# A hand-ordered program with a rewritten task order: 2736 tasks, the same work, another list

## The chip, the cores and the metric

The kernel runs on one core of one Trainium2 chip. The metric is the device time of one execution in microseconds (us), the median of the timed runs. A profile of one more execution shows every instruction on the engines: TensorE (PE for its matmuls, PEld for its weight loads), VectorE (DVE), ScalarE (ACT), GpSimd (POOL), and SyncE (SP), which issues nearly all DMAs.

## The reference

Two blocks in a row, in float32. The first is a recurrence over 768 steps for each of 4 x 8 heads with a 40 x 40 state; the second is a feed-forward layer on its output.

```
for t in range(768):
    y[t] = r[t] @ state
    Sa = state @ a[t]
    state = state * w[t] - outer(Sa, b[t]) + outer(v[t], k[t])
x = y as (3072, 320)
h = x @ w_in                       # 320 -> 2048
out = (h * sigmoid(1.702 * h)) @ w_out   # 2048 -> 320
```

## The kernel before

The sequence is cut into 12 chunks of 64 steps, and the batch into two pairs, which gives 24 units; unit i belongs to chunk i // 2. Within a unit the recurrence becomes matrix work. Cumulated decays come from matmuls (`ps_cum`, `ps_cumc`) or, from unit 4 on, from two scans on DVE (`sums`, L535). Score matrices follow (`ps_A`, `ps_RV`, `ps_N`), then the inverse of a triangular 64 x 64 matrix per head. It takes five `ps_level` steps in a row: a matmul, a copy W (L756), a subtraction E (L758), a 32 x 32 transpose ES (L707) and a spread EX (L716), which feeds the next level. Two corrections (`ps_Q`, `ps_T`), the right-hand sides `ps_B`, the solution `ps_X` and the output `ps_y` come next. `ps_zT` and `ps_rz` carry the state from unit i - 2. The outputs x of the two units of a chunk are written to DRAM (`part_with`, L964) and read back transposed (`get_back`, L970) as xT.

The feed-forward layer takes a chunk when its xT is there: 40 tasks `ps_up` (L1097), a GELU on ACT for each group of ten, and 16 tasks `ps_down` for most chunks. The last two chunks have a product with fewer multiplications (`ps_fast`, L997). The weights arrive as 64-bit words and are first turned into float32 on ACT, DVE and POOL (`weight`, L436): 8 pieces in four DMAs each. That is done during the first 95 us.

What sets the order of all this is a list written into the program. Each piece of work is a task, added by `plan.add` with the engines that it may run on. `ORDER` (L109 to L249) lists all 2736 tasks. An entry such as `113p1` says: task 113, on PE (p; a, d, g and s are ACT, DVE, POOL and SP), and, for a task that uses PSUM, bank pair 1 of four. `Plan.listed` (L89) walks through the list, and `rwkv7_gelu_quick` then emits the tasks one by one (L1169 to L1171). So the list sets four things: the order in which each engine takes its instructions, the engine of each task that may run on several (an EX spread may run on POOL, DVE or ACT), the order of the loads and stores on SP, and the bank pair of each PSUM tile. Each engine runs its own tasks in the list's order; between engines there are only the waits that the data and the buffers need. A load waits on SP until its buffer is free, and everything behind it on SP waits with it. A matmul into a bank pair waits until the last reader of the pair's tile before it is done.

The names that the steps below use: the loads `ak`, `b`, `rv`, `RV`, `time` of a unit (L500), `logw` and `wc` (L495); ahT and khT are the products L624 and L629 of ak with the decays, L626 is that of b, and kh and bh are L632; crossed copies Tc are L804. All matmuls have line L305, that of a helper.

Of the kernel before, what the change touches and what calls it, by code (L numbers as in the profile page):

```python
# [112 lines left out]
344s 92a 115d1 265p2 165d3 114a1 21d 273s 166p1 22d 35s 264p0 23g 116p3 167d1 43s 266a2 36s 118d3 28a 168d1 117d3 169p1 268g  # L113
63s 267a0 270s 119p2 91s 170a1 278g 277s 33s 120d2 287a 122d2 121a 279d 124a2 126p0 171d1 288p3 127a0 31d 172p1 479s 123a2 29d
289a3 51s 125a2 42s 30d 44s 128p2 173a1 45s 129d2 32g 174d1 134p0 175p1 135d0 275s 179a1 290d3 136p2 37a 280g 176d1 180d1 177d
181a1 186p0 291d 138a2 282g 276s 269s 137a2 178d1 146s 281g 187a0 38d 182p1 188p2 183a1 292p0 39d 139d 184p1 283p3 293a0 140s
185d1 284d3 189a2 343s 148a 285p2 315d 46a 190p3 286d2 335p1 141s 191d3 147s 347s 47d 334p2 192p3 61s 336a1 48d 294d0 194a3
348g 338d 337a2 195d 357a 295p2 351g 316p1 297d2 196s 318a1 349d 317a1 62s 296a2 319p1 193d3 358p0 40d 298p3 197s 360d0 41g
346s 361d 299a3 60s 54s 359d0 362p2 341a 300d3 385d 301p3 320a1 350g 364d2 323p1 303d3 355p0 363a2 352g 302a3 356d0 271a 386p3
324d1 365p2 388a3 321p0 64a 387d3 325d1 49d 304p3 322a0 478s 367d2 209p1 50g 309a3 53s 353p0 339s 307d3 210p1 211p1 354d0  # L120
308a3 212p1 366a2 310d3 213p1 305d3 470p0 214p1 272d 72s 368p3 340s 52s 198p2 69s 342d 369a3 215p1 71s 199p2 306a 200p2 370d3
216p1 471a 201p2 65d 202p2 389p3 66d 472a0 474s 217p1 476a 560s 390d3 371p0 67d 482s 218p1 70s 203p2 373d0 68g 219a1 204p2
205p2 477d 220p3 206p2 221p3 222p3 55a 311p1 223p3 80s 224p3 79s 312a1 225p3 372a0 207p2 56d 313p1 226p3 208a2 485d 374p0
314d1 227p3 58d 379a0 228p3 378a0 229p3 57d 326p2 230a3 375d0 59g 393p1 327d2 376a 391p3 394d1 231p2 392a3 558s 232p2 395d1
73a 233p2 81s 483d 381p3 475s 328p1 382a3 76d 380a0 473d 242p3 74d 377a0 481s 492a 78s 75d 243p3 480s 486d 77g 234p2 329d1
244p3 330d1 383p1 245p3 384d1 531d 82a 488p0 487g 235p2 489d0 236p2 237p2 331d 238p2 239p2 396p0 83d 332s 240p2 85d 562s 532p1
708s 241a2 246p3 397d0 559s 534a1 247p3 484d 533a1 84d 535p1 490p0 536a1 86g 398p2 491d0 706s 572a 550p1 253p0 399d2 551a 555s
400d2 561s 254p0 333s 401d 255p0 402s 552a1 564d 493p2 554s 556a 567g 570p1 494d2 705s 248p3 563d 566g 403s 249p3 495d2 498d
571d1 565g 256p0 250a3 496a2 251d3 696p1 497g 557d 539p2 252s 537p3 257p0 538a3 704s 540d2 553d 258p0 701s 611d 697a 499d
573p3 259p0 576a3 784s 574d3 260p0 700s 710d 787s 541d2 261a0 575d3 404p2 698a1 578d 405p2 577g 579d 568p3 711g 500p1 406p2  # L130
569d3 501a1 407p2 262d0 580p3 702a 502d1 408p2 263s 582d3 409p2 503d 410p2 583d 612p0 504a 411p2 584g 613d0 412p2 614d0 413p2
505p1 709d 414a2 426p0 427p0 506d1 428p0 507d1 429p0 699d 430p0 581d3 615p1 703d 431p0 616a1 785s 585p2 432p0 586a2 508d 433p0
434p0 509a 587d2 435p0 588d 448p3 589d 436a0 510p1 590p2 511a1 449p3 592d2 512d1 591a2 415p0 513d 416p0 593d 514a 417p0 594g
418p0 515p1 419p0 516a1 595p2 420p0 517d1 596a2 421p0 518d 422p0 597d2 519a 423p0 598d 424p0 599d 520p1 425a0 437p2 521d1
438p2 523d1 522g 439p2 524d1 440p2 525d1 441p2 442p2 526d1 527p0 718p1 528a0 443p2 719d1 929s 444p2 720d1 529p0 445p2 721d1
446p2 530d0 600p1 723d 447a2 542p0 722d 724g 603d1 604d1 619p2 543d0 605a1 450p3 620a2 606d1 544p0 621d2 601d1 602d 617p2 707s
546d0 451p3 618a2 783s 712d 547g 713d 607p1 725p2 608a1 452p3 609p1 453p3 548s 610d1 727d2 454p3 932s 726d2 622p1 728d 545d0
729a 775p2 455p3 623d1 780s 776a 549s 756d 730p0 624p1 456d3 457d3 731d0 458s 459p3 777a2 778g 732d0 786s 788g 781a 626d1 779s
460p3 625d1 627g 733d 795p2 835d 734a 461p3 735p0 791g 628s 462p3 796d2 736a0 792g 737d0 716p1 738d 463p3 782d 739g 1011s
920p2 757p0 925s 464p3 717d1 758a0 629s 790d 759a0 465p3 789d 740p1 466p3 741a1 921a 742d1 797p0 467d3 760p1 1008s 468d3 800a0  # L140
923d 652p3 761d1 469s 922a2 653p3 926a 798d0 714p2 930s 799d0 654p3 802d 924s 801g 655p3 934d 803a 656p3 836p1 657p3 715d2
658p3 659p3 837d1 762p0 838d1 927d 660p3 763a0 661p3 764p2 662a3 743d 630p1 744d 928s 631p1 765d2 632p1 766d2 804p0 633p1
805a0 634p1 635p1 806d0 745p3 807d 636p1 808a 748d3 637p1 933g 749d3 839p2 750d3 638p1 840a2 1009s 751d3 639p1 935g 809p0
746d3 640a1 641p2 810d0 642p2 793p3 747a 811d0 674p1 812d 794d3 813a 752p0 643p2 753a0 814p3 644p2 815a3 754p0 645p2 816d3
646p2 755d0 647p2 817d 767p3 818a 841p0 768d3 648p2 842a0 649p2 819p3 650p2 820a3 769p0 651a2 821d3 822d 823d 675p1 931s 771d0
824p3 770d0 772g 676p1 936d 827a3 828a3 942p2 829a3 677p1 1153s 830a3 945a2 937d 663p0 773s 825d3 664p0 1156s 943d2 665p0 826a
944d2 999p3 666p0 947d 946g 1000a 1004s 940p2 980d 667p0 948g 774s 668p0 941d2 669p0 670p0 831p2 671p0 1001a3 1002d 1003s
832d2 672p0 1005a 1013d 678p1 673a0 1006d 833p3 843p2 679p1 834d3 1007s 844d2 938p3 845d2 680p1 939d3 846p0 681p1 847d0 949p2
1012g 682d1 848p3 950a2 683d1 1014d 684s 685p0 849d3 1015g 1010s 850d3 1021p1 1016g 951d2 686p0 1024a1 1232s 851d 981p3 1235s
687p0 982a3 952d 852s 1022d1 983a3 953g 1144p2 1023d1 688p0 1026d 1145a 1149s 1025d 1027g 984p3 1059d 689p0 1154s 954p1 853s  # L150
985a3 1147g 690p0 1158d 1148s 955a1 986p3 1146a2 956d1 1150a 957d 691p0 958d 987a3 1151d 988p2 692p0 989a2 1152s 990d2 959p1
693a0 865p3 960a1 694d0 866p3 867p3 695s 961d1 868p3 962d 1028p2 963d 869p3 1029a2 870p3 1157g 871p3 1030d2 1060p0 1031d 872p3
1159d 1032a 873p3 1062d0 874p3 1033p1 1061a0 854p2 875a3 1035d1 855p2 1036d 856p2 1037d 1063p0 857p2 1064d0 858p2 1034a1 964p3
859p2 965a3 1038p0 860p2 966d3 1039a0 861p2 967d 1017p1 1040d0 968a 1041d 862p2 1018d1 863p2 1042g 969p3 864a2 876p0 970d3
# [1098 lines left out]
```

## Time and profile before

| what | value |
|---|---|
| timed runs | 673.79, 675.92, 680.55 us; median 675.92 |
| profiled execution | 673.46 us, of which the span from first to last instruction is 671.7 |
| first matmul, first `ps_up`, end of the last matmul | 3.7, 68.2, 667.8 us |
| granted TensorE clock, mean | 0.991 |
| PE, DVE, ACT, POOL busy | 644.0, 470.7, 318.4, 191.9 us |
| DMA | 69.78 MB, mean 104 GB/s |

The page gives busy time of each engine, and views of the trace cut it by stretches of time, list who waited for whom, and follow the chain of work that ended last. The time of a stretch matters more than the share of the whole: the first 72 us, in which weights load and the first four units have no feed-forward work beside them, differ from the rest.

### The profile page before, as it was taken

What the parts mean: (1) busy time and instruction counts of PE and PEld (TensorE: products, weight loads), DVE (VectorE), ACT (ScalarE), POOL (GpSimd) and SP (SyncE); (2) the same over time, 40 slices, a digit from 0 to 9 for tenths busy, and PEclk for the clock granted to TensorE, in tenths of its full rate; (3) what the DMA queues carried; (4) which work ended last, traced back from release to release, by engine and by line L of the source; (5) the groups of instructions that cost most, each with busy time, mean ns of one, the idle gap of its engine ahead of it and who ended that gap; (6) DMA issues with size and microseconds to landing.
All of it is one profiled execution on the core that took longest, in us unless ns stands there. A gap on an engine that the chain in (4) does not pass through costs nothing.

```text
span 671.7 us, 42976 instructions
## 1 busy us (share of the span) xinstructions
PE 644.0 (96%) x19872; PEld 566.4 (84%) x19872; DVE 470.7 (70%) x956; ACT 318.4 (47%) x658; POOL 191.9 (29%) x214
## 2 busy tenths in 40 slices
PE   5767999999999999999999999999999999999997
PEld 4656988999999898888888888789899787788997
DVE  5688986767867668757775886776757766676505
ACT  3566755534564664574455445454252344353020
POOL 4434344225123123123213620263322333003100
PEclk9699999999999999999999999999999999999999
DMA  7776836205314314432404413422322330210200
GB/s 234 248 239 193 254 125 199 78 14 156 109 45 139 114 43 121 126 112 70 128 14 127 137 48 103 123 67 72 114 86 69 95 90 15 81 44 11 67 21 22
DMA packets 35475, 69.78 MB, mean 104 GB/s; under 512 B 5472, under 2 KB 14816, under 8 KB 35296
## 3 DMA queue, kind: packets, MB, share of 16 engines
q1 hardware_dynamic: 35056, 66.87, 33.0%
q8 instruction: 156, 2.56, 1.5%
q10 hardware_dynamic: 240, 0.16, 0.1%
q14 instruction: 23, 0.19, 0.1%
HBM read 59.15 MB, written 7.86 MB: 100 GB/s over the span
## 4 chain that ended last, share of the span: by engine, by line
PE 93%; DMA 3%; DVE 2%; ACT 1%; issue 1%; SPq 0%; ACTq 0%; DVEq 0%
PE ps_up L305 31%; PE ps_down L305 26%; PE ps_level L305 9%; PE ps_y L305 5%; PE ps_fast L305 5%; PE ps_B L305 4%; PE ps_X L305 3%; PE ps_A L305 2%; PE ps_rz L305 2%; PE ps_N L305 2%; PE ps_RV L305 2%; PE ps_zT L305 1%; DMA time<-in_time 1%; DMA ak<-in_ak 1%; PE ps_cum L305 1%; PE ps_T L305 1%
## 5 line engine op out<-in xcount | busy, mean ns | idle before, releaser
L305 PE MATMUL ps_up<-xT_all,w_sb 64*64 64x256 f32 x3840 | 246.1, 377 | 0.2 <-PE ps_rz L305 0.2
L305 PE MATMUL ps_down<-w_sb,g 64*64 64x320 f32 x2560 | 201.3, 430 | 0.0
L305 PEld LDWEIGHTS ps_up<-xT_all,w_sb 64*64 64x64 f32 x3840 | 167.6, 133 | 17.7 <-DVE B L899 0.5
L305 PEld LDWEIGHTS ps_down<-w_sb,g 64*64 64x64 f32 x2560 | 114.0, 133 | 28.6 <-issue 0.3
L1107 ACT ACTIVATE g<-ps_up 128x1024 f32<-128x1024 f32 x48 | 49.1, 1026 | 62.2 <-PE ps_up L305 61.9
L756 ACT COPY W<-ps_level 128x512 f32<-128x512 f32 x56 | 32.7, 587 | 67.1 <-PE ps_level L305 53.0
L714 POOL TENSOR_TENSOR EX<-ES,quads 128x512 f32<-128x512 f32 x29 | 38.0, 1310 | 92.5 <-DVE ES L707 77.7
L305 PEld LDWEIGHTS ps_level<-W,EX 64*64 64x64 f32 x2560 | 56.8, 134 | 5.3 <-ACT EX L712 0.2
L758 DVE TENSOR_TENSOR E<-two,ps_level 128x256 f32<-128x256 f32 x80 | 33.3, 417 | 38.7 <-ACT W L756 22.6
L305 PE MATMUL ps_level<-W,EX 64*64 64x64 f32 (+1 forms) x2560 | 54.3, 217 | 0.0
L712 ACT ACTIVATE EX<-ES,quads 128x256 f32<-128x256 f32 x74 | 33.7, 503 | 35.8 <-DVE ES L707 31.1
L624 POOL TENSOR_TENSOR ak<-ak,FT 128x512 f32<-128x512 f32 x17 | 22.0, 1297 | 80.0 <-DMA ak<-in_ak 59.3
L305 PEld LDWEIGHTS ps_level<-PT,EX 64*64 64x64 f32 x1280 | 32.5, 144 | 9.1 <-issue 2.7
L305 PE MATMUL ps_level<-PT,EX 64*64 64x64 f32 (+2 forms) x1280 | 34.6, 242 | 5.5 <-DVE EX L728 2.0
L707 DVE STREAM_TRANSPOSE ES<-E 128x256 f32<-128x256 f32 x80 | 35.0, 441 | 4.1
L305 PE MATMUL ps_y<-M,bh 64*64 64x104 f32 (+1 forms) x768 | 35.2, 247 | 0.7 <-issue 0.4
L305 PE MATMUL ps_y<-RV,kh 64*64 64x104 f32 (+1 forms) x768 | 34.9, 247 | 0.2 <-issue 0.2
L912 DVE TENSOR_TENSOR M<-ps_X,later 128x832 f32<-128x832 f32 (+1 forms) x24 | 23.8, 991 | 12.1 <-PE ps_X L305 12.0
L896 ACT COPY B<-ps_B 128x416 f32<-128x416 f32 (+1 forms) x29 | 14.5, 498 | 37.1 <-PE ps_B L305 37.0
L305 PEld LDWEIGHTS ps_y<-RV,kh 64*64 64x64 f32 x768 | 28.5, 133 | 2.0 <-issue 0.4
L714 POOL TENSOR_TENSOR T<-ES,quads 128x512 f32<-128x512 f32 x9 | 11.5, 1277 | 64.6 <-DVE ES L707 64.6
L305 PEld LDWEIGHTS ps_B<-RV,A 64*64 64x64 f32 x768 | 24.7, 135 | 5.2 <-issue 1.2
(156 smaller groups left out, 1205.0 us busy)
## 6 DMA issues: line engine op xcount, KB each, us to landing
rv<-in_rv SPq DMA_DIRECT2D x48, 160.0 KB
ak<-in_ak SPq DMA_DIRECT2D x48, 160.0 KB
time<-in_time SPq DMA_DIRECT2D x24, 320.0 KB
xT_all<-x_dram SPq DMA_DIRECT2D x48, 160.0 KB
wc<-in_wc SPq DMA_DIRECT2D x20, 264.0 KB
logw<-in_w SPq DMA_DIRECT2D x24, 160.0 KB
RV<-in_v SPq DMA_DIRECT2D x24, 160.0 KB
b<-in_b SPq DMA_DIRECT2D x48, 80.0 KB
```

Source lines behind the costliest of these rows:

```text
L305: nc.tensor.matmul(o, lhsT, rhs, start=start, stop=True, skip_group_check=True)
L624: plan.add(R, {"DVE": 690.0, "POOL": 1270.0, "sbuf": True}, lambda t: of(t.engine).tensor_mul(ahT(), ahT(), FT_of(i)), reads=T("ak", "FT") ...
L707: plan.add(rank, dve(256), lambda t: nc.vector.transpose(ES(n), source(t)), writes=[key("ES", n, 6)], **reads)
L712: nc.scalar.activation(dst[:, :, h], ES(n), ACT.Copy, scale=quads[:, h, :1])
L714: of(t.engine).tensor_mul(dst, ES(n).unsqueeze(2).to_broadcast([128, 8, 2, 32]), quads.unsqueeze(1).to_broadcast([128, 8, 2, 32]))
L756: plan.add(rank, any2(512), lambda t: copy(t.engine)(tiles_of(W(n + 1)), blocks(psum(t, ""), 64)), writes=[key("W", n + 1, 5)], pair=pair)
L758: plan.add(rank, dve(256), lambda t: nc.vector.tensor_sub(tiles_of(E(n + 1)), every(two32, [128, 2, 4, 32]), blocks(psum(t, ""), 64)[:, :, ...
L896: plan.add(R, any2(4 * wide), lambda t: copy(t.engine)(dst(), some(psum(t, "")[:, :, :208])), writes=[("Bv", i)] if x and c > 0 else T("B" ...
L912: plan.add(R + 1, dve(8 * wide), lambda t: nc.vector.tensor_tensor(M_of(i)[:, :, :wide].rearrange("p (j b) n -> p b j n", b=2), some(psum( ...
L1107: plan.add(-45, {"ACT": 1030.0, "table": "gelu"}, lambda t: nc.scalar.activation(g_of(c * NQ + q).rearrange("p q b n -> p b q n"), psum(t, ...
```

## The change

Only the text of `ORDER` changes. It was searched for with the mean of six draws of late loads and scattered DMA packets as its target, and the words that came with it speak of units 4 to 22. The text differs from its first line to its last but a few entries. The first three lines of both:

```diff
-0s 7s 5s 8s 9s 6s 3a 88p3 16s 1s 87p1 100p2 89a3 12s 102a 95d 14s 90a1 93d 10s 101d2 98p3 97d 24s 94d 96d 103p1 11s 4a 99d3
-15s 132p0 105d1 17s 142p2 106d 143p3 133d0 13s 107p0 144a3 18s 2s 104a1 149g 109d0 130p1 34s 25s 108a0 26s 150d 158a 110p3
-145a2 131a1 152g 159p2 112d3 156p1 160a2 151g 111a3 161d2 162d 153d 19a 154p2 157d1 345s 163p3 155d2 27s 113p1 274s 164a3 20d
...
+0s 7s 5s 158a 8s 9s 6s 3a 87p3 1s 88p2 16s 89a2 10s 90a3 100p2 95d 102a 93d 12s 101d2 98p0 14s 97d 18s 94d 4a 99d0 103p2 11s
+96d 15s 132p0 105d2 142p1 17s 106d 104a2 143p2 133d0 24s 107p0 13s 144a2 2s 130p2 149g 109d0 34s 131a2 25s 108d0 145a1 151g
+26s 150d 110p0 153g 112d0 159p2 111a0 152g 156p1 160d2 19a 161d2 154p0 162d 345s 157d1 163p3 27s 274s 155d0 113p1 164a3 20d
...
```

Here 10 is the load of `ak` for unit 1, 12 and 14 its `rv` and `time`, 11 its `b`; 16, 15, 17 and 18 are the four DMAs of weight piece 0, and 24 is the first of piece 1; 149 and 151 are ahT and khT of unit 1, 150 is the product of its b, 152 and 153 are kh and bh; 108 and 111 are copies of unit 0's first levels, 159 is `ps_N` of unit 1 and 160 a copy of its result; 158 is the preset of unit 1 (L680).

Counted over the whole text: 303 tasks have another engine (DVE to ACT 99, ACT to DVE 86, DVE to POOL 50, POOL to DVE 39, ACT to POOL 18, POOL to ACT 11). 259 tasks have another bank pair. On PE 639 of 1076 tasks stand at another rank, on SP 204 of 269. DVE has 807 tasks in place of 831, POOL 165 in place of 147, ACT 419 in place of 413.

More of the change, by code (lines that the diff above doesn't have):

```diff
@@ L114 @@
[L114 to L130, printed above, removed]
@@ new lines @@
+1092p1 1198d2 1208p3 918d0 1093p1 1209a3 1378s 1196d2 1094p1 1095p1 1195a 1372s 1212p0 1200p2 1096p1 1213a0 1201d2 1210p3
+1214d0 1202p2 1097p1 1211a3 1376s 1203d2 1078p0 1229a 1373s 1098p1 919s 1215p2 1099a1 1241p3 1216d2 1079p0 1080p0 1242d3
+1081p0 1082p0 1217p1 1383d 1262p3 1219d1 1384g 1379s 1083p0 1084p0 1218d1 1385g 1111p2 1264d3 1112p2 1230d 1263a3 1085p0
+1086p0 1087p0 1220d 1388p3 1088a0 1113p2 1447p1 1283d 1114p2 1448a 1452s 1115p2 1389d3 1284p0 1265d 1116p2 1266d 1117p2 1122p3
+1285d0 1381d 1449a1 1451s 1118p2 1453a 1221s 1286d0 1119p2 1120p2 1287p0 1121a2 1123p3 1288d0 1267p0 1291p1 1222s 1269d0
@@ new lines @@
+1314p2 1413a1 1315p2 1308p0 1509a3 1414d1 1316p2 1415d 1317p2 1416d 1318p2 1486p1 1309p0 1488d1 1310p0 1489d 1487a1 1311p0
+1510d3 1490g 1319p2 1312a0 1417p1 1324p3 1422d1 1325p3 1418d1 1320p2 1423d1 1419g 1321p2 1322p2 1420a1 1326p3 1421d1 1323a2
+1491p0 1607g 1327p3 1492d0 1328p3 1329p3 1493d0 1424p1 1494d 1330p3 1425d1 1495g 1614p2 1331p3 1615d2 1825s 1332p3 1616d2
+1426p0 1333p3 1617a2 1427d0 1496p1 1334a3 1439p2 1500d1 1346p0 1497d1 1502d1 1498a 1440d2 1347p0 1619d 1441p2 1501d1 1499a1
+1503p1 1335p3 1442d2 1609g 1504a1 1336p3 1443d2 1337p3 1608g 1505p1 1511p2 1618g 1506d1 1348p0 1444d 1512a2 1681s 2425g 1349p0
@@ new lines @@
+1525s 1629d 1826s 1691p2 1613d1 1363p3 1692d2 1817a 1630d 1658p2 1660p1 1818a0 1830d 1820s 1364p3 1659a2 1824s 1661d1 1822a
+1537p0 1538p0 1365a3 1539p0 1366d3 1540p0 1662d1 1693p2 1631p3 1696a2 1904s 1541p0 1632a3 1694d2 1689p1 1907s 1695d2 1542p0
+1367s 1698d 1697g 1543p0 1690d1 1699a 1544p0 1545p0 1633d3 1546p0 1678d 1526p2 1547a0 1732p1 1700p3 1634d 1527p2 1635d 1528p2
+1529p2 1702d3 1530p2 1829d 1701a3 1531p2 1734a1 1819d 1532p2 1703d 1636p3 1733d1 1704g 1533p2 1638d3 1534p2 1639d 1637a3
+1535p2 1640d 1705p1 1536a2 1548p0 1707d1 1549p0 1708d 1735p3 1706a1 2422d 1709g 1550p0 1736a3 1551p0 1552p0 1641p1 1559p2
@@ new lines @@
+1856a0 1752p2 1753p2 1858d 1754p2 1589d3 1859a 1924p1 1590d3 1755p2 1955d 1591s 1860p0 1926d1 1761p3 1927d 1861a0 1756p2 1928g
+1757p2 1925a1 1862d0 1758p2 1863d 1759p2 2053g 1956p0 1760a2 1762p3 1958d0 1763p3 1764p3 1864g 1929p1 1765p3 1931d1 1766p3
+1932d 1865p2 1933d 1767p3 1870a2 1768p3 1930d1 1957a0 1769p3 1871d2 1934p1 1868d2 1770p3 1935a1 1794p0 1866d2 1771a3 1867g
+1936d1 1937d 1772p1 1869d2 1773p1 1938d 1959p2 1774p1 2054d 1960a2 2129s 1939p3 1775p1 1941d3 1776p1 1940d3 1872p2 1777p1
+1942d 2062p3 1873d2 1778p1 2055g 2427g 2426g 2064d3 1779p1 2063d3 1780p1 2065d3 1874p2 1781p1 1875d2 1783p3 1782a1 2047d
@@ new lines @@
+2183p2 1980p0 2184d2 2351s 2153p1 2279g 1981p0 2154a1 1986p3 1987p3 2155d1 1988p3 2156d 1989p3 2278d 2157a 1982p0 1983p0
+2079p1 1984a0 1990p3 2081d1 1991p3 2082d 1992p3 2080d1 2158p2 1993p3 2160d2 2083a 1996p1 2159d2 1997p1 1994p3 2267d 2161d
+2084p2 1995a3 1998p1 2086d2 1999p1 2162d 2000p1 2085a2 2001p1 2087d 2163p0 2088a 2018p2 2165d0 2166d 2089p3 2164d0 2002p1
+2093a3 2007p0 2008p0 2090d3 2003p1 2092d3 2091g 2004p1 2095d3 2005p1 2167d 2094a3 2019p2 2006a1 2277d 2009p0 2096p3 2010p0
+2097d3 2286p1 2098p3 2011p0 2289d1 2512s 2012p0 2099d3 1815s 2013p0 2287d1 2111p3 2288d1 2291d 2290g 2168p1 2014p0 2292g
@@ new lines @@
+2197s 2284p0 2295d2 2369g 2033p3 2285d0 2515s 2294a2 2028s 2296d 2330p0 2297g 2034p3 2331d0 2332p0 2367g 2402p2 2358g 2333d0
+2511s 2298p1 2404a2 2035p3 2403a2 2300d1 2513s 2301d 2036p3 2299d1 2302a 2334d0 2507p1 2303p2 2037d3 2508a 2198p0 2038d3
+2199p0 2305d2 2200p0 2306d 2509a1 2201p0 2307g 2304a2 2370p3 2202p0 2347a 2372d3 2203p0 2204p0 2371a3 2348d 2205p0 2206p0
+2405p3 2373d 2359p1 2406a3 2587s 2374d 2207p0 2209p2 2517d 2586s 2208a0 2210p2 2516d 2211p2 2039s 2212p2 2360d1 2375p3 2213p2
+2376d3 2214p2 2215p2 2377d3 2220p1 2378d 2221p1 2379d 2308p0 2216p2 2310d0 2380p3 2311d 2222p1 2382d3 2312a 2217p2 2309d0
@@ new lines @@
+2218p2 2223p1 2383d 2219a2 2313p0 2381d3 2384g 2224p1 2314d0 2225p1 2319a0 2226p1 2315g 2227p1 2317a0 2385p2 2318a0 2228p1
+2316a0 2387d2 2229p1 2388d 2386a2 2320p3 2525p0 2389g 2321a3 2242p2 2527d0 2230a1 2526d0 2231p3 2530d 2232p3 2528d0 2531g
+2233p3 2322p0 2234p3 2323d0 2390p1 2510g 2335p0 2394a1 2235p3 2393a1 2336d0 2236p3 2237p3 2238p3 2391d1 2337p0 2395d1 2392g
+2396a1 2239p3 2338d0 2519g 2514s 2240p3 2563d 2407p1 2241a3 2243p2 2339d0 2408a1 2520d 2340g 2409p3 2564p1 2410d3 2397p0
+2244p2 2398a0 2411d3 2566d1 2399p0 2529g 2245p2 2341s 2565a1 2400d0 2518g 2246p2 2523p3 2412p1 2342s 2247p2 2585s 2413d1
@@ new lines @@
+2610d 2542p1 2607a0 2641p3 2544d1 2433p2 2545d 2642a3 2434p2 2543d1 2435p2 2439p0 2546d 2611p1 2436p2 2613d1 2437p2 2614d
+2440p0 2438a2 2615d 2441p0 2442p0 2612d1 2443p0 2547p3 2616p1 2549d3 2444p0 2550d 2445p0 2618d1 2551a 2446p0 2548d3 2447p0
+2617a1 2448p0 2619d 2552p2 2620d 2449a0 2450p3 2553d2 2451p3 2557d2 2452p3 2554a 2594d 2621p1 2453p3 2558a2 2623d1 2559p0
+2555a2 2454p3 2624d 2556a2 2455p3 2560d0 2456p3 2625a 2622d1 2561p2 2457p3 2562d2 2626p1 2461p0 2630d1 2574p2 2629a1 2458p3
+2575d2 2459p3 2632a1 2462p0 2627d1 2460a3 2463p0 2631d1 2464p0 2645p2 2628a 2576p3 2646a2 2643p1 2647d2 2472d 2465p0 2644a1
```

209 lines of the change are left out of this document (93 added, 116 removed).

## The prediction

> **What bounds the kernel now.** I read the busy table first, then the stretches, then who waited for whom, then the chain that ended last.
>
> ```profile
> PE 644.0 (96%) x19872; PEld 566.4 (84%) x19872; DVE 470.7 (70%) x956; ACT 318.4 (47%) x658; POOL 191.9 (29%) x214
> PE 93%; DMA 3%; DVE 2%; ACT 1%; issue 1%; SPq 0%; ACTq 0%; DVEq 0%
> ```
>
> TensorE is busy 96% of the span, and 93% of the chain that ended last is TensorE. No other engine comes near. The stretches say where the other 4% lies:
>
> ```profile
> 0.00:25.00 25.00, 14.66 (x429) 13.17 (x433) 15.14 (x26) 10.28 (x29) 10.76 (x43) 0.93 0.80 253
> 25.00:45.00 20.00, 14.48 (x500) 13.00 (x492) 14.45 (x25) 12.36 (x32) 8.84 (x6) 0.83 0.76 233
> 45.00:72.00 27.00, 20.39 (x860) 18.42 (x861) 23.99 (x48) 17.92 (x40) 12.51 (x8) 1.00 0.61 186
> ...
> 300.00:350.00 50.00, 50.00 (x1565) 41.88 (x1561) 39.48 (x90) 24.21 (x47) 11.91 (x13) 1.00 0.27 81
> 350.00:400.00 50.00, 50.00 (x1504) 42.12 (x1500) 36.88 (x69) 24.09 (x43) 20.29 (x19) 1.00 0.37 103
> 400.00:450.00 50.00, 50.00 (x1590) 40.71 (x1584) 36.53 (x75) 26.67 (x60) 14.08 (x13) 1.00 0.31 88
> ```
>
> The columns are the stretch, its length, busy time of PE, PEld, DVE, ACT and POOL, the granted clock and the DMA share. TensorE idles 10.3, 5.5 and 6.6 us in the three stretches before 72 us. Ten stretches of 50 us from 100 to 600 us add up to 499 busy of 500. The waits of TensorE agree: the long ones (3.7, 3.0, 1.5 us) are all in the front.
>
> ```profile
> PE ps_cumc L305 <- POOL logw L372: 3.7, 1, 3.7
> PE ps_A L305 <- DVE ak L624: 3.0, 1, 3.0
> PE ps_level L305 <- DVE EX L728: 2.0, 2, 1.5
> ```
>
> A busy row can hide short gaps, so I also took the distance between the first matmul starts of neighbouring tasks. One ps_up task (8 matmuls) steps 432 ns, one ps_down task 1079, one level of an inversion 464. These steps hardly depend on the neighbour. At the lowest tenth of each kind's steps all 1076 TensorE tasks make 621.5 us. The first matmul starts at 3.7 and the last ends at 667.8, so stalls take 667.8 - 3.7 - 621.5 = 42.6 us. The first ps_up starts at 68.2 us with 31.6 us of steps before it, so 32.9 of the 42.6 lie ahead of that point, and 9.7 in the 600 us behind it. After the last matmul come 3.9 us (evictions, stores).
>
> **The change, part by part.** It rewrites the list and nothing else. I counted both lists. No matmul is added or removed: the 621.5 us stand. 639 of 1076 TensorE tasks change rank, by 2.2 places on average; 204 of SP's 269 tasks change rank; 303 evictions and elementwise tasks change engine; 259 tasks have another PSUM bank pair.
>
> *Engine changes.* DVE loses 24 tasks (831 to 807), POOL gains 18 (147 to 165), ACT 6. By the rows' means (an EX spread is 693 ns on DVE, 1310 on POOL, two of 503 on ACT) DVE falls by about 10 us and POOL rises by about 13. All of it lies beside TensorE, which stays full in stretches where DVE is busy 66 to 79% and POOL 17 to 41%. The cover is that idle 20 to 30% of DVE; without it each moved spread would show up to 0.6 us on its level. GELU table reloads fall from 29 to 27, 1.28 us each on ACT, which is 47% busy: nothing on the path.
>
> A price of this move is in the trace: scans of 0.68 us take up to 3.12, while POOL works on a 2.97 us integer add from 77.97.
>
> ```profile
> 78.38 3.12 DVE L538 TENSOR_TENSOR_SCAN wc<-starts,wc 128x264 f32<-128x264 f32 x1
> 81.43 0.68 DVE L539 TENSOR_TENSOR_SCAN wc<-starts,wc 128x264 f32<-128x264 f32 x1
> ```
>
> Summed over DVE, 46 instructions are stretched by 24.6 us in all, beside 181 us of POOL tasks: 0.14 us per us of POOL work. Thirteen more us of POOL make about 1.8 us more of stretched DVE, spread over 600 us. I take 0 on the path, and 1.8 as its end. [...]
>
> *Middle order and banks.* For each TensorE task I counted how much TensorE work stands in the list between it and the work that feeds it, minus the durations of the evictions between (rows again: W copy 0.59 on ACT, 0.68 on DVE; E 0.42; transpose 0.45; M 1.02; GELU 1.02). This is the spare time of a link; waiting in an engine's queue is not in it. Behind the first ps_up, before has 24 links with under 0.5 us to spare, 92 under 1 us and 235 under 2; after has 34, 104 and 242. Most are PSUM bank pairs taken again soon after an eviction. The 9.7 us of stalls scaled by these counts become 13.7, 11.0 or 10.0. I take the second, +1.3 us, because the instruction that can be queued ahead of an eviction lasts 0.4 to 1.0 us, so links under 1 us are those which one queued instruction makes late. Ends: -9.7 (every stall gone) and +13.8 (each of the 34 tightest waits for one 0.69 us DVE instruction: 23.5 in place of 9.7).
>
> *Loads.* SP is in order, so a load is issued no earlier than what stands before it. Behind the first ps_up the smallest leads from possible issue to first use move from 4.3 to 4.6 us for ak and from 3.2 to 3.8 for the x stores, and for time fall from 15.8 to 9.7. The median lead of ak goes from 5.7 to 7.6. In before, no wait of TensorE behind the first ps_up has a load as its cause, so I take 0. The gain end is inside the -9.7 above; a late ak would be worth up to its longest wait on POOL in the trace, 10.9 us, less the 4.6 us lead, 6.3.
>
> *Front.* The 53 TensorE tasks ahead of the first ps_up are the same 53, 31.6 us, nearly in the same order. What can move is when the chain gets there. ak of unit 1 is issued three places earlier, but ps_N of unit 1, at 20.14, also needs b of unit 1, whose negated product on DVE starts at 18.81 when the load is in. In both lists that load has the same tiles ahead of it. It took 1.11 us in place of 0.68 while POOL multiplied kh at 18.52 to 19.38; an earlier ak lets POOL finish sooner. I take -0.4 us; the ends are -1.2 (the idle time of TensorE before ps_N) and +3.2 (the links here with less than nothing to spare go from -13.9 to -17.1 us in sum).
>
> **The sum** is made against the profiled execution, 673.46 us: a span of 671.7 and 1.8 around it. 673.46 - 0.4 + 1.3 = 674.4. The profiled execution is quicker than all three timed runs (673.79, 675.92, 680.55). The middle of these four times is 674.9, 1.4 above the profiled one. A median of after should stand as far off: 674.4 + 1.4 = 675.8, against a median of 675.92 before.
>
> **The rivals.**
>
> *1. The clock stays up in the front: 671.8.* The granted clock is 0.50 from 21.7 to 31.9 us, though TensorE is busy 8.8 of these 10.2:
>
> ```profile
> 18.00:21.70 3.70, 2.24 (x104) 1.00 0.90 301
> 21.70:31.90 10.20, 8.81 (x220) 0.50 0.83 260
> ```
>
> The chain that ended last holds 8.0 us of TensorE work in that window, so at full clock it ends 4.0 us sooner: 675.8 - 4.0. For it: the earlier loads thin out the idle time just ahead. Against it: the order of TensorE there is the same. The reverse, a second such window between 42 and 62 us, would cost 3.2 to 6.2 us, the chain's TensorE work in each half of that stage. [...]
>
> *2. The middle closes up: 666.1.* If the order does what its name says and late loads no longer stall TensorE, the 9.7 us go: 675.8 - 9.7. Faster by over 1% (under 669.2) needs 6.6 of them. Against it: the gaps left are many of tens of ns, the largest 0.6 us, and after has more tight links.
>
> *3. Bank links turn into waits: 688.3.* This is the one that ends slower. TensorE runs its list in order, so a bank freed late stops everything behind it. With one 0.69 us DVE instruction before each of the 34 tightest links: 675.8 - 1.3 + 13.8. It is slower by over 1% (682.7) from 0.52 us per link, (9.7 + 8.2) / 34. For it: 303 moved evictions, 259 moved banks. Against it: before has 24 such links and waits 0.4 us for each even if all its stalls are put on them.
>
> *4. The same list in effect.* All moves lie under TensorE work, and only the front's load order is felt: within 2 us of 675.9. That is within my forecast's case and counted with it.
>
> **How the numbers follow.** Forecast with rival 4: 0.60. Rival 1: 0.15. Rival 2: 0.10. Rival 3: 0.15. A measurement of this kernel tells about 1% from no change. The forecast's case and rival 1 stay within 1% (669.2 to 682.7), so 0.75 for the same, 0.10 faster, 0.15 slower. The range reaches to 668 (rival 1 and about a third of the middle's stalls) and to 684 (two clock windows, or rival 3 at 0.55 us per link), leaving out about 0.1 at each end.
>
> **What would show it.** The first ps_up starts within 2 us of 68.2. TensorE stays at 49.5 or more of 50 in every stretch from 100 to 600 us; if one falls under 48.5, rival 3 is at work, and the waits of TensorE will name DVE or ACT evictions. POOL's busy time rises to about 205 us and DVE's falls to about 462. The clock row shows whether the half-rate slice near 25 us is still there, and a second one there would be the rest of a slower time. The forecast is wrong if TensorE's idle time behind 75 us changes by more than 4 us, or if a load appears among its waits there.

## The result, and the profile after

The changed kernel takes 681.0 us (median of 22 runs, 675.33 to 685.51) against 676.05 us for the kernel before (22 runs on the same chips, 670.44 to 682.43). The ratio is 1.0078, with a 95% interval of 1.0051 to 1.0105: a loss of 0.8%, about 5 us, where no change was forecast. Ratios leave disturbed runs out, so they can differ a little from the quotient of two medians. The profiled execution took 680.16 us, with a span of 678.4.

First the busy table of the changed kernel and its chain that ended last:

```profile
PE 646.5 (95%) x19872; PEld 560.1 (83%) x19872; DVE 457.8 (67%) x921; ACT 314.8 (46%) x669; POOL 202.0 (30%) x232
PE 90%; DVE 6%; issue 2%; DMA 1%; ACT 1%; SPq 0%; DVEq 0%; ACTq 0%
```

VectorE (DVE) lost 13 us of work and POOL gained 10, close to what was forecast. But VectorE's share of the chain rose from 2% to 6%: it has less work, and more of it now decides the end. The stretches (columns as in the prediction) say where:

```profile
0.00:25.00 25.00, 14.61 (x401) 13.06 (x405) 15.26 (x26) 9.37 (x27) 12.08 (x44) 0.86 0.75 233
25.00:45.00 20.00, 13.85 (x527) 12.40 (x519) 15.05 (x25) 13.29 (x34) 10.49 (x7) 0.92 0.80 258
45.00:72.00 27.00, 19.84 (x873) 17.60 (x877) 23.92 (x42) 17.97 (x46) 10.68 (x7) 1.00 0.61 187
...
250.00:300.00 50.00, 48.94 (x1505) 43.11 (x1500) 37.37 (x81) 25.10 (x52) 12.29 (x13) 1.00 0.38 112
300.00:350.00 50.00, 50.00 (x1548) 42.81 (x1541) 32.64 (x69) 26.39 (x54) 17.00 (x17) 1.00 0.30 87
350.00:400.00 50.00, 48.20 (x1402) 38.06 (x1395) 34.43 (x63) 23.21 (x43) 14.35 (x15) 0.97 0.36 106
...
450.00:500.00 50.00, 48.98 (x1496) 38.45 (x1492) 36.15 (x73) 19.88 (x44) 19.63 (x20) 1.00 0.31 93
```

The front is as before: the first ps_up starts at 68.16 us (68.20 before), and one 10.24 us window at half clock lies there in both (from 18.1 us here, from 21.7 before). Three stretches of the middle are no longer full, and the middle one also lost clock. TensorE's waits behind 72 us name what ended the idle time:

```profile
PE ps_B L305 <- DVE B L896: 1.8, 1, 1.8
PE ps_N L305 <- issue: 1.2, 2, 0.8
PE ps_level L305 <- DVE EX L714: 0.6, 1, 0.6
```

By the measure of the prediction (each step of TensorE beyond the lowest tenth of its kind) the stalls behind 72 us are 16.2 us in place of 9.3: all of the 6.7 us between the two profiled executions.

The largest one is the first row. VectorE's timeline ahead of it, and POOL's in the same microseconds (start, duration, engine, line, operation, tiles, form):

```profile
357.78 4.73 DVE L958 TENSOR_TENSOR x<-zr,FT 128x128 f32<-128x128 f32 x4
362.43 1.82 DVE L850 TENSOR_TENSOR zr<-zraw,wz 128x320 f32<-128x320 f32 x1
364.18 0.58 DVE L896 COPY B<-ps_B 128x416 f32<-128x416 f32 x1
```

```profile
357.92 3.15 POOL L994 TENSOR_TENSOR extra<-w_sb 128x640 f32<-128x640 f32 x2
361.03 1.33 POOL L714 TENSOR_TENSOR EX<-ES,quads 128x512 f32<-128x512 f32 x1
362.32 1.59 POOL L994 TENSOR_TENSOR extra<-w_sb 128x640 f32<-128x640 f32 x1
```

The four multiplies for the x of a unit usually take 0.90 us together on VectorE, 0.28 us each with a little overlap. This is such a row of the kernel before:

```profile
371.83 0.90 DVE L958 TENSOR_TENSOR x<-zr,FT 128x128 f32<-128x128 f32 x4
```

For unit 12 (task 1444) they take 4.73. They end at 358.12, 359.66, 361.22 and 362.50, each 0.15 us after a POOL instruction (357.97, a short one ahead of the rows shown, then 359.52, 361.07 and 362.35). The update of zr behind them, usually 0.48, takes 1.82 and ends 0.34 us after the next one. By these rows the two engines ran in turns: a multiply of 0.28 us ended only behind an instruction of POOL's of 1.3 to 1.6 us, three times in a row, and then the update of zr once more.

Behind this queue stands the eviction (the copy that empties a PSUM bank) of the first half of B of unit 13 (L896, task 1514), and TensorE's second ps_B needs its bank:

```profile
364.81 0.59 PE L305 MATMUL ps_B<-RV,A 64*64 64x104 f32 x16 [1.80 <-DVE B L896]
```

In the kernel before, x of unit 12 is on POOL at that place, and POOL's weight sums (L994) come later:

```profile
355.33 1.71 POOL L958 TENSOR_TENSOR x<-zr,FT 128x128 f32<-128x128 f32 x4
```

Soon after the wait the granted clock falls to a half for 3.41 us, in the midst of the run:

```profile
362.60:366.20 3.60, 1.80 (x76) 1.39 (x72) 2.15 (x2) 1.97 (x6) 1.31 (x1) 1.00 0.35 93
366.27:369.68 3.41, 3.41 (x35) 1.87 (x31) 1.79 (x3) 2.39 (x3) 0.00 (x0) 0.50 0.36 126
```

A second, smaller place of the kind is at 455 to 459 us, where a spread of EX and a product on VectorE are stretched (0.69 to 1.64 and 0.68 to 2.02 us) beside a POOL queue of khT and the two halves of T4, which the change moved there from VectorE. TensorE lost 0.9 and 0.7 us. A third loss, 1.0 us at 266, is marked "issue": TensorE stopped amid the matmuls of one task, whose data it had. I took it at first for a third such meeting; it proved to be something else (below).

### The profile page after: what moved, and what is told of

Its sections match the earlier page's. It is cut to its first block, busy times and chain, and to the rows that moved or that the text cites. A ratio compares the mean times of both kernels' runs of the same rounds, so it can differ in the third digit from the quotient of the medians.

```text
span 678.4 us, 42915 instructions
## 1 busy us (share of the span) xinstructions
PE 646.5 (95%) x19872; PEld 560.1 (83%) x19872; DVE 457.8 (67%) x921; ACT 314.8 (46%) x669; POOL 202.0 (30%) x232
## 4 chain that ended last, share of the span: by engine, by line
PE 90%; DVE 6%; issue 2%; DMA 1%; ACT 1%; SPq 0%; DVEq 0%; ACTq 0%
PE ps_up L305 29%; PE ps_down L305 25%; PE ps_level L305 9%; PE ps_y L305 5%; PE ps_fast L305 5%; PE ps_B L305 4%; PE ps_X L305 3%; PE ps_A L305 2%; PE ps_N L305 2%; PE ps_RV L305 2%; PE ps_rz L305 1%; DVE x L958 1%; PE ps_zT L305 1%; PE ps_cum L305 1%; PE ps_T L305 1%
## 5 line engine op out<-in xcount | busy, mean ns | idle before, releaser
L305 PE MATMUL ps_up<-xT_all,w_sb 64*64 64x256 f32 x3840 | 243.0, 378 | 0.0
L305 PE MATMUL ps_down<-w_sb,g 64*64 64x320 f32 x2560 | 197.8, 431 | 0.0
L305 PEld LDWEIGHTS ps_up<-xT_all,w_sb 64*64 64x64 f32 x3840 | 170.4, 133 | 17.6 <-issue 0.9
L305 PEld LDWEIGHTS ps_down<-w_sb,g 64*64 64x64 f32 x2560 | 109.6, 134 | 36.0 <-issue 1.8
L714 POOL TENSOR_TENSOR EX<-ES,quads 128x512 f32<-128x512 f32 x32 | 41.9, 1308 | 122.7 <-DVE ES L707 121.2
L712 ACT ACTIVATE EX<-ES,quads 128x256 f32<-128x256 f32 x74 | 33.4, 502 | 21.9 <-DVE ES L707 21.7
L802 ACT COPY Tc<-ps_level 32x64 f32<-32x64 f32 x112 | 22.8, 203 | 38.0 <-PE ps_level L305 17.0
L912 DVE TENSOR_TENSOR M<-ps_X,later 128x832 f32<-128x832 f32 (+1 forms) x24 | 23.8, 992 | 18.9 <-PE ps_X L305 18.6
L896 ACT COPY B<-ps_B 128x416 f32<-128x416 f32 (+1 forms) x31 | 15.1, 492 | 35.0 <-PE ps_B L305 35.0
L632 POOL TENSOR_TENSOR kh<-time,G 128x320 f32<-128x320 f32 x19 | 17.5, 919 | 42.6 <-PE ps_y L305 22.5
L632 POOL TENSOR_TENSOR bh<-time,G 128x320 f32<-128x320 f32 x21 | 18.3, 873 | 39.3 <-PE ps_y L305 30.6
L305 PEld LDWEIGHTS ps_y<-RV,kh 64*64 64x64 f32 x768 | 27.0, 133 | 2.8 <-DVE M L912 1.5
```

The costliest lines, as they stand in the source:

```text
L305: nc.tensor.matmul(o, lhsT, rhs, start=start, stop=True, skip_group_check=True)
L632: plan.add(R + 4, {"POOL": 870.0, "DVE": 490.0, "sbuf": True}, lambda t, n=n, dst=dst: of(t.engine).tensor_mul(dst(i)[:, :, :D], by_head(t ...
L712: nc.scalar.activation(dst[:, :, h], ES(n), ACT.Copy, scale=quads[:, h, :1])
L714: of(t.engine).tensor_mul(dst, ES(n).unsqueeze(2).to_broadcast([128, 8, 2, 32]), quads.unsqueeze(1).to_broadcast([128, 8, 2, 32]))
L802: copy(t.engine)(dst, src[:, u, :, f])
L896: plan.add(R, any2(4 * wide), lambda t: copy(t.engine)(dst(), some(psum(t, "")[:, :, :208])), writes=[("Bv", i)] if x and c > 0 else T("B" ...
```

## The experiments

**The theories.** L: the engine choices of the change make VectorE and POOL meet on the path. O: the order and the banks have thinner cover for every eviction, and the places seen are only where that happens to show. Later a third suspect came up, F: TensorE's instructions themselves arrive late.

To compare profiles I sorted the gaps of over 0.3 us between two starts on TensorE behind 72 us (outside half-clock windows) into two kinds: those that end 1.1 to 1.8 us after a packet of the instruction queue and are marked "issue" or not marked ("late packets"), and all others ("late results"; a wait for a load is counted here). One wait of 1.0 us each in e6 and in e11 (both have the order of before) also ends 1.4 us after a packet, but the trace puts it down to the load of xT, whose last part landed 0.13 us before TensorE went on; these two are late results.

**The two halves of the change**

*e1: order, banks and DMA list of the change, engines of before.* All 303 engine letters are put back, as in

```diff
-1444d 1050g 1159g 2426g 2427g 2055g
+1444g 1050a 1159d 2426d 2427d 2055d
...
```

> The order, the bank pairs and SP's list of the changed kernel, but each task on the engine that it had before. Theory L (VectorE and GpSimd stretch each other, and the new engine choices put long stretches on TensorE's path): the stall of 2.0 us at ps_up beside x of unit 12 is gone, the stalls of TensorE behind 72 us fall from 16.2 to 9 to 11 us, ratio to before 1.000 to 1.003. Theory O (the new order and banks leave less cover): the stalls stay at 14 to 17 us and the ratio at 1.006 to 1.010.

*e2: the kernel before with the 303 engines of the change*, the same edit the other way.

> The other half: the order, banks and SP's list of the kernel before, with the engine choices of the changed one. Theory L: slower than before by 3 to 7 us, ratio 1.004 to 1.010, and VectorE instructions of two to five times their usual length stand ahead of TensorE's waits. Theory O: ratio 0.998 to 1.002, stalls of 9 to 11 us behind 72 us.

e1 took 696.37 us, ratio 1.0309 (1.0257 to 1.0361), e2 692.2 us, ratio 1.0264 (1.0203 to 1.0325). Each half alone costs three to four times the loss of the whole change. TensorE's waits in e1 are spread over many engines and tiles:

```profile
PE ps_level L305 <- DVE EX L714: 1.6, 2, 1.4
PE ps_N L305 <- DVE Tc L802: 1.6, 1, 1.6
PE ps_Q L305 <- DVE Tc L802: 1.1, 1, 1.1
PE ps_level L305 <- ACT W L756: 1.0, 1, 1.0
```

Late results make 16.6 us in e1 and 16.2 in e2, against 1.4 in before. So neither "the order" nor "the engines" has a price of its own: a list of engines fits one order. Both theories missed in both runs, by far, so this says nothing for L or O yet. It shows that halves are the wrong edit here; single meetings have to be tried.

**Taking meetings away**

*e3: three tasks back to the engine of before:* x of unit 12, and the halves of T4.

```diff
-1444d 2426g 2427g
+1444g 2426d 2427d
```

> The changed kernel with three tasks back on their old engine: x of unit 12 on GpSimd (it was moved to VectorE), the two T4 subtractions on VectorE (they were moved to GpSimd). Theory L: the stalls near 362 and 455 us are gone, 3.5 and 1.5 us, so the ratio to before falls from 1.008 to 1.000 to 1.003. Theory O: those two places mend, but as much comes back elsewhere, ratio 1.006 or more.

*e4: the changed kernel again, one profile.*

> The changed kernel once more, for a second profile of it. Theory L: x of unit 12 takes 4 to 5 us on VectorE again and TensorE stalls 2 us behind it, since the same two lists meet there in every execution. If the stall were chance, it would be somewhere else or absent, and the time 3 us or more lower.

e3 took 678.68 us, ratio 1.0035 (0.9999 to 1.0070). The wait at 363 us is gone, late results fall to 2.1 us, and the ratio is just above the range of L. e4 (679.17 us) has it again at the same place, 1.8 us on the same eviction, with late results of 4.5 us: the meeting is in the program and not a chance of one execution. The half-clock window did not follow it there.

*e5: x stays on VectorE, POOL's queue is moved away.* Tasks 2425, 2421 and 2424 go behind task 1686; no engine changes.

```diff
-1444d ... 2425g ... 2421g ... 1620g ... 2424g ... 1686g
+1444d ... 1620g ... 1686g 2425g 2421g 2424g
```

> The changed kernel with every engine choice left as it is; only three weight sums (L994, tasks 2425, 2421 and 2424) are put later in POOL's own order, behind task 1686, where POOL had 12 us without work in the changed kernel's profile. Theory L (VectorE's operation with two SBUF inputs and POOL's run in turns when they meet, and at 357.8 us this lies on the path): x of unit 12 stays on VectorE and takes 0.9 to 1.9 us in place of 4.73 (only the spread of EX, 1.33 us on POOL, still starts beside it), the 1.80 us wait of TensorE on the eviction of B is gone, and the time falls by 2 to 4 us against the changed kernel, to 677 to 679 us, as in the run with the three tasks put back. Theory M (x is simply too long for VectorE at that place, whatever POOL does): x of unit 12 keeps 3 us or more, the wait stays over 1 us, and the time stays at 680 to 682.

*e6: the meeting put into the kernel before.*

```diff
-1620a ... 1444g ... 2421g ... 2424g ... 2425g
+1444d 2425g 2421g 1620g 2424g
```

> The kernel before with the one meeting of the changed kernel put into it: x of unit 12 (task 1444) on VectorE, and POOL's tasks 2425, 2421, 1620 (the spread of EX, from ScalarE) and 2424 right behind it in POOL's order; all else as before. Theory L: x takes 4 to 5 us in place of 0.9, the eviction of B (task 1514) comes about 2 us late, TensorE waits 1.5 to 2.5 us on it, and the time rises by 1.5 to 4 us (ratio 1.002 to 1.006). Rival (what costs is the order searched as a whole; the meeting at 357.8 us is harmless where the order around it has cover): x may be as long, but TensorE's wait on the eviction of B stays under 0.5 us and the time stays within 1 us of before (ratio 0.9985 to 1.0015).

*e7: six tasks back.*

```diff
-1444d 1050g 1159g 2426g 2427g 2055g
+1444g 1050a 1159d 2426d 2427d 2055d
```

> The changed kernel with the engine of six tasks put back to that of before, those that met on the path at the three places where the trace lost time: 1444 (x of unit 12) to POOL; 1050 (T0 of unit 9) to ScalarE and 1159 (khT of unit 10) to VectorE; 2426 and 2427 (T4) and 2055 (khT of unit 18) to VectorE. Order, banks and DMA list stay those of the change. Theory L: the stalls near 265, 363 and 458 us are all under 0.5 us, stalls behind 72 us are 10 to 12 us in all (before 9.3, changed 16.2), and the time is 675 to 678 us, ratio to before 0.999 to 1.003. Rival O (the order has thinner cover everywhere, and the meetings are only where it happens to show): the time stays at 679 to 682, ratio 1.005 to 1.009, with stalls at other places.

VectorE's timeline in e5, with only the spread of EX (1.32 us) left beside x:

```profile
367.96 2.03 DVE L958 TENSOR_TENSOR x<-zr,FT 128x128 f32<-128x128 f32 x4
369.91 0.48 DVE L850 TENSOR_TENSOR zr<-zraw,wz 128x320 f32<-128x320 f32 x1
371.95 0.59 DVE L896 COPY B<-ps_B 128x416 f32<-128x416 f32 x1 [1.56 <-PE ps_B L305]
```

L had 0.9 to 1.9 us for x. Now the eviction waits for TensorE and not TensorE for the eviction. Nothing was done to x but to move POOL's work, so theory M (x is too long there anyway) falls. And in e6, VectorE, POOL and TensorE:

```profile
360.01 5.71 DVE L958 TENSOR_TENSOR x<-zr,FT 128x128 f32<-128x128 f32 x4
365.64 0.58 DVE L896 COPY B<-ps_B 128x416 f32<-128x416 f32 x1
```

```profile
359.63 3.11 POOL L994 TENSOR_TENSOR extra<-w_sb 128x640 f32<-128x640 f32 x2
362.70 1.32 POOL L714 TENSOR_TENSOR EX<-ES,quads 128x512 f32<-128x512 f32 x1
363.99 1.58 POOL L994 TENSOR_TENSOR extra<-w_sb 128x640 f32<-128x640 f32 x1
```

```profile
366.27 0.59 PE L305 MATMUL ps_B<-RV,A 64*64 64x104 f32 x16 [2.22 <-DVE B L896]
```

e6 took 681.72 us beside 677.8 for before, ratio 1.0048 (1.0012 to 1.0083): the wait (2.2 us) and the time as L had them, and x even longer than the 4 to 5 us expected; here, too, each of the four multiplies ends 0.15 us after a POOL instruction. One meeting can cost about half a per cent in the order of before, too, though the profile also has 3.6 us of late packets, so that not all of the loss need be the wait.

The times of e5 and e7 did not follow. e5 took 685.5 us, ratio 1.0096 (1.0055 to 1.0137); e7 681.22 us, ratio 1.0023 (0.9986 to 1.0061), and its profile had 18.9 us of stalls where L had 10 to 12. Late results were low (2.2 and 1.7 us), but the waits marked "issue" had grown: 9.2 and 8.0 us of late packets, against 3.6 in e6 on the same chip. e7 also shows that putting a task back has a price: its T4 halves, on VectorE again but in the new order, stand ahead of an eviction that TensorE needs.

```profile
456.19 1.55 DVE L994 TENSOR_TENSOR extra<-w_sb,extra 128x640 f32<-128x640 f32 x2
457.65 0.91 DVE L694 COPY_PREDICATED PT<-within,ps_N 128x256 f32<-128x256 uint32 x2
458.46 0.42 DVE L697 COPY P<-ps_N 128x256 f32<-128x256 f32 x1
```

```profile
459.02 0.66 PE L305 MATMUL ps_up<-xT_all,w_sb 64*64 64x256 f32 x8 [1.13 <-DVE P L697]
```

**Late packets**

The page lists, for both kernels, a queue of instructions:

```profile
q8 instruction: 156, 2.56, 1.5%
```

156 packets of 16,384 bytes, for 39,744 matmuls and weight loads: one per 255 instructions, or per 4.1 us of the middle. That they bring TensorE's instructions is read from this count and from the waits below. In the changed kernel one packet was served from 264.30 to 265.20 us, amid the data packets of q1:

```profile
q1 hardware_dynamic: 118, 0.15, 71.0%
q8 instruction: 1, 0.02, 5.1%
```

and TensorE, which had stopped after 10 matmuls of a task, went on 1.58 us after that landing:

```profile
266.78 0.40 PE L305 MATMUL ps_N<-b,ak 40*64 40x64 f32 x12 [0.82 <-issue]
```

The same task is held up so in nine of the eleven profiles with the change's order, by 0.7 to 1.6 us (not in e1 and e4). There the DMA engines are busy. The stretch from 262 to 266 us, first of the changed kernel and then of the kernel before (the last two columns are the DMA share and GB/s):

```profile
262.00:266.00 4.00, 3.96 (x118) 3.82 (x110) 2.44 (x5) 0.59 (x1) 2.48 (x2) 1.00 0.68 186
```

```profile
262.00:266.00 4.00, 4.00 (x142) 3.36 (x138) 3.90 (x9) 1.39 (x3) 0.43 (x1) 1.00 0.02 6
```

So my first reading of this place, a meeting of x of unit 8 with POOL, was wrong. Over all profiles, of 68 waits behind 72 us that show as over 0.3 us between two starts (outside half-clock windows) and are marked "issue", 62 end 1.1 to 1.8 us after a packet of this queue; with a packet each 4.1 us, chance would give about one in six. So it is well shown that in these runs TensorE waits for its instructions. That the data loads are what makes a packet late is another question. To test F, the loads of `ak`, `b`, `rv` and x are cut in three kernels.

*e8, e9, e10: shorter loads in the kernel before, in the changed one, and in e7.* From unit 6 on, `ak`, `b` and `rv` are loaded in 8 of 40 rows, and x is fetched back in 13 of 64 from pair 5 on; the rest of the operands is stale, so most of the output is not what the reference gives.

```diff
                 for p in rows:
+                    if i >= 6 and len(rows) == 2:
+                        p = slice(p.start, p.start + 8)
                     dst = of(i)
...
-                nc.sync.dma_start(xT_of(c)[h, p].rearrange("q k n -> q (k n)"), drams[i].rearrange("(q k) n -> q (k n)", q=64))
+                q = slice(0, 13 if c >= 5 else 64)
+                nc.sync.dma_start(xT_of(c)[h, p][q].rearrange("q k n -> q (k n)"), drams[i].rearrange("(q k) n -> q (k n)", q=64)[q])
```

> The kernel before with shorter loads: from unit 6 on ak, b and rv are loaded only in 8 of their 40 rows per half (L508), and from pair 5 on x comes back only in 13 of 64 rows (L974), so that most of the output is computed from stale numbers; every instruction of every engine and every DMA issue stays. It is the base for the next two. A new suspect is behind it, theory F: TensorE's own instructions come by DMA (queue q8, 156 packets of 16 KB), a wait marked 'issue' ends 1.2 to 1.7 us after such a packet landed, and with the data loads in the way the packet comes late. F: waits of over 0.3 us that end so (4 with 1.5 us in the profile of before) go under 1 us in all; time 1 to 4 us under that of before (ratio 0.994 to 0.999). Rival (loads and instruction packets have nothing to do with the waits): time within 1 us of before, the waits marked 'issue' as before.

> The changed kernel with the same shorter loads as e8 (same rows left out). Theory L with F: waits on VectorE's late results stay at 3.5 to 5 us (4.35 in the profile after, 1.39 before), waits for instruction packets fall from 2 to 4 us to under 1 us; it is 2 to 4 us slower than e8. Rival O (the searched order is short of cover everywhere): 5 us or more slower than e8, with waits at new places. Rival 'loads alone' (the whole loss is late packets): within 1 us of e8.

> The changed kernel with the six tasks of e7 back on the engines of before, and the same shorter loads as e8. L with F: both costs are gone, so waits on results stay at 1 to 2.5 us, waits for packets under 1 us, and the time is within 1.5 us of e8. Rival O: 2 to 5 us slower than e8, as e7 was 1.5 to 3.5 us slower than before, with long waits marked neither by VectorE and POOL in turns nor by a packet.

*e11: the kernel before again, one profile beside them.*

> The kernel before once more, for a second profile beside these runs. All theories: 671 to 682 us. F: waits for instruction packets 1 to 4.5 us in all behind 72 us (1.5 in the first profile, 4.6 in e6, which has the same order), less than in the changed kernel's order on the same chip (2.1 to 9.2 in five profiles). If it has 8 us of them too, these waits are the chip's and not the order's.

e8 took 673.56 us, ratio 0.9971 (0.9943 to 0.9999), and its late packets are 0.8 us. Both are as F had them, but the two profiles of before with full loads have 1.5 and 0.8 us, so this run doesn't show that shorter loads bring the packets sooner. e11, the second of these two profiles, took 675.38 us. e9 took 680.35 us, ratio 1.0076 (1.0041 to 1.0110). Its late packets fell only to 1.7 us, and the same task ps_N is held up as before, by 0.9 us in this view:

```profile
PE ps_N L305 <- issue: 1.4, 2, 0.9
```

The DMA engines are still 60% busy from 262 to 268 us there, and in e4, which has no wait at this place, 56%. So that the loads hold up this packet is argued and not shown. Late results stayed in e9 (5.2 us, the same 1.8 us wait on B among them), and it is 6.8 us slower than e8: more than L with F had, and as much as O had, though the largest wait is the old one. "Loads alone" is out: with the loads cut, the change costs as much as with them. e10 took 679.65 us, ratio 1.0076 (1.0048 to 1.0104), 6.1 us slower than e8 where L with F had at most 1.5. That is a miss. Its stalls are 14.1 us against 8.0 in e8: 2.6 more of late packets, 1.6 more of late results (the new 1.1 us wait of e7 is in it), 1.9 more in small gaps. By this run O looked better than L.

**One meeting at a time**

e7 and e10 had put tasks back that were no part of the 363 us meeting, and paid for it. The last three change as little as can be.

*e12: one task of 2736 edited.*

```diff
-1444d
+1444g
```

*e13: e12, and the halves of T4 stay on POOL, behind task 2518, where VectorE was idle.*

```diff
-1444d ... 2427g 2426g ... 2518g
+1444g ... 2518g 2427g 2426g
```

*e14: the changed kernel beside them.*

> The changed kernel with one task changed: x of unit 12 (task 1444) on POOL as before. Theory L: the one wait of 1.8 to 2.1 us near 363 us is gone (and with it the half-rate window that followed it in two of three profiles), waits on results behind 72 us fall from 4.4 to 2.0 to 2.8 us; 2 to 4 us under the changed kernel run beside it. Rival O (each engine change only moves the loss, as it looked in e7 and e10): within 1.5 us of the changed kernel beside it, with a new wait of 1 us or more.

> As e12, and POOL's two halves of T4 (tasks 2427 and 2426) stay on POOL, but behind task 2518, where VectorE had nothing to do in the changed kernel's profile, so that neither place where the two met on the path is left. Theory L: waits on results behind 72 us 1.0 to 1.8 us (before: 1.4), and 3 to 5 us under the changed kernel beside it; ratio to before 1.000 to 1.004, what is left being late packets and the closer order. If VectorE is what is late there in any case: the waits near 457 stay over 0.5 us and the time is that of e12.

> The changed kernel once more, timed on the same chip beside e12 and e13. All theories: ratio to before 1.005 to 1.011, waits on results behind 72 us 4 to 5 us, at 363 and 457 us.

e14 took 683.84 us, ratio 1.0139 (1.0090 to 1.0188), more than the 1.005 to 1.011 expected. e12 took 677.12 us, ratio 1.0006 (0.9969 to 1.0042): one letter takes most of the loss away. That all of it goes is not shown, since e3 and e13, which hold the same edit and one more, have 1.0035 and 1.0039. The 6.7 us between e14 and e12 are also more than the 2 to 4 that L had, and more than the 3.6 us between the stalls of their profiles; the rest has no explanation here. TensorE's waits behind 72 us and the stretch from 350 us in e12, where x is on POOL:

```profile
PE ps_N L305 <- issue: 1.6, 2, 1.1
PE ps_level L305 <- DVE EX L714: 0.6, 1, 0.6
```

```profile
350.00:400.00 50.00, 50.00 (x1521) 41.79 (x1517) 30.77 (x63) 24.96 (x45) 18.08 (x21) 1.00 0.36 106
```

```profile
358.53 1.95 POOL L958 TENSOR_TENSOR x<-zr,FT 128x128 f32<-128x128 f32 x4
360.44 3.05 POOL L994 TENSOR_TENSOR extra<-w_sb 128x640 f32<-128x640 f32 x2
```

The stretch is full again and at full clock. No wait on B is left; x and the weight sums follow each other on one engine and cannot meet. e13 took 677.37 us, ratio 1.0039 (0.9999 to 1.0079), no better than e12: late results fell further (2.3 to 1.6 us), but of the two waits near 457 only the second went; in the first the spread of EX meets khT on POOL, not T4.

In e14 the half-clock window came again, 1.0 us after the wait on B had ended:

```profile
365.93:369.34 3.41, 3.41 (x56) 2.20 (x51) 1.79 (x3) 2.81 (x3) 0.00 (x0) 0.50 0.47 164
```

The profiles side by side (us, stalls behind 72 us as above):

| profile | all stalls | late results | late packets | half clock mid-run |
|---|---|---|---|---|
| before, e11 | 9.3, 9.8 | 1.4, 2.4 | 1.5, 0.8 | no, no |
| changed, e4, e14 | 16.2, 13.7, 16.8 | 4.4, 4.5, 4.6 | 2.1, 2.2, 3.6 | yes, no, yes |
| e12, e13 | 13.2, 12.0 | 2.3, 1.6 | 2.3, 3.7 | no, no |
| e6 (before with the meeting) | 16.3 | 5.4 | 3.6 | no |
| e5, e7 | 21.4, 18.9 | 2.2, 1.7 | 9.2, 8.0 | no, no |
| e8, e9, e10 (short loads) | 8.0, 15.6, 14.1 | 1.4, 5.2, 3.0 | 0.8, 1.7, 3.3 | no, yes, no |

No kernel here that does all the work beats the one before.

## Why the prediction was wrong, step by step

**Engine changes: the step that failed.** The prediction said: "I take 0 on the path, and 1.8 as its end", with the idle 20 to 30% of VectorE as cover. The amounts were right (POOL 202.0 where about 205 was forecast, DVE 457.8 where about 462 was) and even too high in sum: all stretching of VectorE beside POOL fell from 24.6 us in 46 instructions to 21.8 in 37. But the price was not proportional to POOL's work and not spread over 600 us. It was paid where a chain of small two-input operations on VectorE met a POOL queue without a pause, ahead of an eviction. There x and zr took 6.55 us in place of 1.38, TensorE lost 2.0, and in three of four profiles of the change's order with this wait (the changed kernel, e9, e14; not e4) a half-clock window followed, in which its tasks took 1.5 us more in e14. e12 and e6 show it from both sides: away, the median is 1.3 us above that of before; put in, 3.9 us are lost (late packets may have a share in that). An idle share of 25% over a stretch is no cover for an eviction in one queue.

**Middle order and banks: mechanism right, measure blind.** +1.3 us was taken from counts of tight links. The gaps under 0.3 us agree with that size: what is left of the stalls after late results, late packets and the half-clock window (1.5 us, as in e14) is 6.4 and 6.6 us in the two profiles of before and 7.0 to 8.2 in the three of the changed kernel. But the link that broke was tight in both lists: three ps_up tasks (1.30 us) stand between the two ps_B of unit 13 before as after, less an eviction of 0.59. The prediction noted that "waiting in an engine's queue is not in it"; that was the term that mattered. A list of spare times without the queue of the evicting engine can't tell these two programs apart.

**Rival 3** is what happened in kind: a bank freed late stops TensorE. It came at one place with 1.8 us, and not at 34. The prediction's own signs for it fired: a stretch under 48.5 us (48.20), the wait naming a VectorE eviction, and TensorE's stalls behind 72 us up by more than 4 (idle time in the busy rows alone goes from 1.3 to 4.3 us, since these rows hide short gaps).

**Rival 2** did not come. Its 666.1 was also worked out too high: the forecast of 675.8 already held 1.3 us more of stalls, so with all 11.0 gone the working gives 664.8.

**Front.** -0.4 us was taken; the two profiles differ by 0.04 at the first ps_up. Over all profiles this start lies between 63.9 and 72.1 us. The two earliest have no half-clock window ahead of it (e8 and e13) and the latest has three (e3), but e10 has none and starts at 69.4, so the windows are not all of it. No run here shows that the change moves this start. Rival 1 did not come: the window is there. That idle time just ahead of it brings the window is not shown: in before TensorE idled 2.96 us from 6.66 us, and at most 1.2 us at a time in the 12 us before the window. One reading of the prediction is to be put right: ak of unit 1 stands two places earlier among SP's tasks, not three.

**Loads.** 0 was taken, as no wait named a load. No wait of the changed kernel behind 72 us names one, but a cost was there in another form: the changed kernel has 2.1 to 3.6 us of late packets, before 0.8 to 1.5. That is a term which the prediction did not have at all. That the moved loads hold the packets up is not shown (e9).

**The sum as measured:** stalls behind 72 us rise from 9.6 (mean of two profiles) to 15.6 (three), 6.0 us: 2.6 late results, 1.5 late packets, about 1.0 half clock (1.5 in two of three), 0.9 small gaps. The medians differ by 5.0.

**What stays open.** e12's profile still has 13.2 us of stalls, 3.6 more than before, while its time is only 1.3 us longer; its interval, and the times of e3 and e13, leave open whether 0 or 3 us remain. Why late packets reached 8 to 9 us in e5 and e7 was not settled, nor why e10 stayed 6 us behind e8; that the tasks put back made new meetings is shown for one wait of 1.1 us only. Why the half-clock window follows the wait in some executions was not tried.

## What to carry to other kernels

When work moves to POOL, don't price it by busy shares: go to each VectorE chain ahead of an eviction that TensorE needs, and ask what POOL has queued in those microseconds. Here each of the four small multiplies of x ended behind one POOL instruction, and x cost 4.73 us in place of 0.90. And undo single entries, not whole halves: of 303 moved tasks one carried most of the loss (e12), while putting back all 303 lost 3%.

## What the runs showed of the hardware

- In the changed kernel and in e6 VectorE and POOL ran in turns: four multiplies of 0.28 us each (x of unit 12, two inputs) each ended 0.15 us after a POOL instruction of 1.3 to 1.6 us (the first one in the changed kernel after one of 0.74). Together they took 4.73 and 5.71 us in place of 0.90.
- In the middle of a run TensorE had waits marked "issue", in which nothing else that the profile shows held it, one of 1.6 us in e7 (ps_y). Of 68 of over 0.3 us, 62 ended 1.1 to 1.8 us after a 16 KB packet of the queue q8 had landed. The one at 266 us in the changed kernel, 1.58 us after its packet, comes amid data loads (DMA share 0.68); that the loads make the packet late is not shown.
- The granted clock fell to 0.50 for 3.41 us in mid-run, 1.0 to 1.5 us after a single wait of 1.8 us, in three of the four profiles with that wait in the change's order (the changed kernel, e9, e14; not e4), and in no profile without such a wait. In e6, whose wait was 2.2 us, it did not.
